# K turned by VectorE for other units, and q0 of four heads in two halves, in a sliding-window attention kernel

## The chip, the cores and the metric

The kernel runs on one core of a Trainium2 chip. A core has a matrix engine (TensorE, "PE" in the profile, its weight loads "PEld"), a vector engine (VectorE, "DVE"), a scalar engine (ScalarE, "ACT"), a general engine (GpSimd, "POOL") and a queue engine (SyncE, "SP") that issues nearly all transfers here. Transfers are carried by 16 DMA engines, which work beside the five. The engines run at the same time, each through its own instructions in order, and wait for each other by semaphores. SBUF is the memory on the core, PSUM the one that TensorE writes.

The metric is the time of one execution on the device, in microseconds (us). Eight executions of the kernel before lie between 185.21 and 186.71, with a median of 185.62.

## The reference

```python
B, Sq, D = 8, 32, 1024
Hq, Hkv, Sk, Dh = 32, 4, 8192, 128
W = 2048                                   # the last W positions of the cache
rep = Hq // Hkv                            # 8 query heads share one K and V
q = (x @ wq)  as [B, Hq, Sq, Dh]
k = k_cache[:, :, Sk - W:, :],  v = v_cache[:, :, Sk - W:, :]   each repeated rep times
p = softmax(q @ k^T * Dh**-0.5)
out = ((p @ v) as [B, Sq, Hq*Dh]) @ wo
```

All tensors are bf16. K and V of one batch entry and one KV head are 2048 x 128, 512 KB each.

## The kernel before

**Units and slots.** The work is cut into 32 units, one for each pair of KV head g and batch entry b: units 0 to 7 have g = 0, units 8 to 15 have g = 1, and so on. A unit has 256 queries (8 heads of 32) against 2048 keys. It is worked in four slots of 512 keys, so slot 4u is the first slot of unit u, and there are 128 slots. In a slot TensorE makes the scores (L467, four matmuls into s_ps), ScalarE takes their exponentials (L469, pT), and TensorE makes the product with V of a slot that lies two back (L478, eight matmuls into o_ps). V has a column of ones beside it in the tiles va, so that o_ps also holds the sum of the exponentials. At a unit's end VectorE takes the reciprocal of that sum (L415), scales o_ps (L420, two instructions of 128 columns) and transposes the result in blocks into OT (L422).

**Side work.** TensorE has other matmuls to do between these: q of the next KV head (q_pieces, L275, eight heads in 16 pieces), the output projection of a finished one (o_pieces, L295), and transposes of K. A dictionary, made by side_plan, says which piece is put behind which slot. Q_SLOTS and O_SLOTS give each group's first and last slot, and the function spread lays the pieces evenly over them. The order of every engine's instructions is the program's order.

**K comes turned in three ways.** The scores need K with its 128 columns on the partitions.

- Units in PE_T (0 to 4): K is loaded as it lies (L193) and turned by TensorE against an identity (L236, sixteen transposes in four pieces during the unit before, one piece behind each slot), then copied from PSUM by VectorE (L238). Unit 0's K is turned during the start (L368).
- Units in V_T (5, 8, 11, ... 29): K is loaded as it lies. VectorE transposes blocks of 32 x 32 (L251, four instructions), and sixteen moves of 32 partitions by 512 elements put the blocks in place. An entry holds the unit whose loading also loads this K, the slots of the four transposes, the first and last slot of the moves, and how many of the sixteen moves GpSimd makes (L261). VectorE makes the rest (L259). It is 12 for unit 5 and 16 for the others.
- All other units, 18 of them: a transposing DMA (L196), in two halves of 256 KB.

**Loads.** SP issues all of them in program order. load_unit loads a unit's K and V and then, where W_AT names this unit, pieces of wq or wo, in the order of the list self.weights. Loads are asked for about five units ahead; SP waits at an instruction until its target buffer is free. wq of one KV head comes in two tiles, each with half of the rows of the product's inner dimension and all eight heads; a DMA of 512 KB then has rows of 2 KB.

**The start.** x is loaded and transposed, q of KV head 0 (q0) is computed chunk by chunk as the chunks of wq land (L375): all 256 columns (8 batch entries of 32) for the first six chunks, and the first 128 columns for the last two. The 16 matmuls that are left are made behind slots 0 and 1 (q_rest). Four copies put the columns of batch entry 0 into QT (two by ScalarE, two by VectorE), four more by VectorE put the rest.

**V.** VectorE copies V of each unit from its landing tile into one of three tiles va (L409), at the unit's first slot.

Of the kernel before, what the change touches and what calls it, by code (L numbers as in the profile page):

```python
# [9 lines left out]
ALU = mybir.AluOpType  # L10
# [5 lines left out]

RL_LIMIT = 1.0e22
RL_MIN = 1.0e-10
Q_CUT = 6
N_WARM = (8, 0, 0)  # L20
VA_ROW = 160
V_HALVES = 30

PE_T = (0, 1, 2, 3, 4)

V_T = {5: (2, (5, 6, 8, 10), 10, 17, 12),
       **{u: (u - 4, range(4 * u - 16, 4 * u - 12), 4 * u - 13, 4 * u - 4, 16) for u in (8, 11, 14, 17, 20, 23, 26, 29)}}
W_AT = (3, 3, 4, 4, 8, 8, 9, 9, 11, 12, 13, 13, 14, 15, 16, 16, 18, 19, 19, 20, 22, 22, 23, 24, 25, 26, 28, 28)

Q_SLOTS = {1: (17, 31), 2: (38, 54), 3: (69, 83)}  # L30
O_SLOTS = {0: (54, 71), 1: (84, 101), 2: (99, 123), 3: (124, 143)}


# [71 lines left out]
class Fast:  # L105
# [50 lines left out]
    def load_wq(self, g, half, cuts=(2, 2)):  # L156
# [8 lines left out]
                                   in_=self.wq[:, g * GW:(g + 1) * GW].rearrange("(p c) n -> p c n", p=P)[:, c0:c0 + n, :])  # L165
        return [lambda i=sum(cuts[:k]), n=n: piece(i, n) for k, n in enumerate(cuts)]

    def load_wo(self, gq):

        def piece(i):  # L170
            if i == 0:
                self.wo_t[gq] = self.wp.tile([self.P, 4, self.D], BF16, name="wo_sb", tag="w")
            r0 = gq * 4 * self.Dh
            self.nc.sync.dma_start(out=self.wo_t[gq][:, 2 * i:2 * i + 2, :],
                                   in_=self.wo[r0:r0 + 4 * self.Dh, :].rearrange("(p c) n -> p c n", c=4)[:, 2 * i:2 * i + 2, :])
        return [lambda i=i: piece(i) for i in range(2)]
# [30 lines left out]
    def load_unit(self, ui):  # L207

        if ui < len(self.units):
            if ui not in V_T:  # L210
                self.load_k(ui, None if ui in PE_T else 0)
            self.load_v(ui, self.nc.sync)
            if ui not in V_T and ui not in PE_T:
                self.load_k(ui, 1)
        for u, at in V_T.items():
            if at[0] == ui:
                self.load_k(u)
        for p, at in zip(self.weights, W_AT):
            if at == ui:
                p()  # L220

# [17 lines left out]
    def kv_pieces(self, ui):  # L241


        nc, P, KT = self.nc, self.P, self.KT
        st = {}

        def blocks(i):
            if i == 0:
                st["kb"] = self.kbp.tile([P, KT, P], BF16, name="kb")
            sl = slice(i * KT // 4, (i + 1) * KT // 4)  # L250
            nc.vector.transpose(out=st["kb"][:, sl, :], in_=self.k_raw[ui][:, sl, :])  # L251

        def move(k, d):
            if k == d == 0:
                self.kT[ui] = self.kvt.tile([P, KT, P], BF16, name="kTv", tag="kv")
            out = self.kT[ui][d * 32:(d + 1) * 32, :, k * 32:(k + 1) * 32]
            in_ = st["kb"][k * 32:(k + 1) * 32, :, d * 32:(d + 1) * 32]
            if d >= V_T[ui][4] // 4:
                nc.vector.tensor_copy(out=out, in_=in_)  # L259
            else:  # L260
                nc.gpsimd.tensor_scalar(out=out, in0=in_, scalar1=1.0, scalar2=1.0, op0=ALU.mult, op1=ALU.mult)  # L261
        return [lambda i=i: blocks(i) for i in range(4)], [lambda k=k, d=d: move(k, d) for k in range(4) for d in range(4)]
# [4 lines left out]
    def q_pieces(self, g):  # L267
        nc, P, DC = self.nc, self.P, self.DC
        st = {}

        def piece(hl, i):
            if i == 0:
                st["ps"] = self.ps_m.tile([P, 512], FP32, name="q_ps", tag="m")
            for c in range(i * DC // 2, (i + 1) * DC // 2):
                nc.tensor.matmul(st["ps"][:, 0:self.NQ], lhsT=self.wq_t[g, i][:, c % (DC // 2), hl * P:(hl + 1) * P],  # L275
                                 rhs=self.xT[:, c, :], start=(c == 0), stop=(c == DC - 1))
            if i == 1:
                nc.vector.tensor_copy(out=self.q_view(g)[:, :, hl, :],  # L278
                                      in_=st["ps"][:, 0:self.NQ].rearrange("p (b s) -> p b s", b=self.B))
        return [lambda h=h, i=i: piece(h, i) for h in range(self.rep) for i in range(2)]  # L280

    def o_pieces(self, g, t, cuts=(512, 512), st=None):

# [28 lines left out]
    def start(self):  # L312
# [15 lines left out]
        self.load_k(0, 1)  # L328
        self.load_v(0, nc.sync)
        self.load_k(1)  # L330
        self.load_v(1, nc.sync)
        self.weights = []
        for g in range(self.Hkv):
            if g + 1 < self.Hkv:
                self.weights += self.load_wq(g + 1, 0) + self.load_wq(g + 1, 1)
            if g:
                self.weights += self.load_wo(2 * g - 2) + self.load_wo(2 * g - 1)
        self.weights += self.load_wo(2 * self.Hkv - 2) + self.load_wo(2 * self.Hkv - 1)
        for ui in range(2, 4):
            self.load_unit(ui)  # L340
        for v in self.va:
            nc.gpsimd.memset(v[:, :, self.Dh:self.VW], 1.0)
        nc.gpsimd.memset(self.ones_c[:, :], 1.0)
        def warm_up(n):
            for i in range(n):
                nc.tensor.matmul(warm[:, :], lhsT=one(1.0, [P, P], BF16), rhs=one(1.0, [P, 512], BF16), start=True, stop=True)
        warm_up(N_WARM[0])


        def x_turn(half, pl, tag):  # L350
# [4 lines left out]
            for i, copy in ((0, nc.vector.tensor_copy), (1, nc.scalar.copy)):  # L355
# [2 lines left out]

        x_turn(0, self.ps_m, "m")
        x_turn(1, self.ps_s, "s_ps")  # L360
        qs = [pl.tile([P, 2, self.NQ], FP32, name="q0_ps", tag=tag)
              for pl, tag in ((self.ps_o, "o_ps"), (self.ps_o, "o_ps"), (self.ps_m, "m"), (self.ps_m, "m"))]
        KT = self.KT
        tp = None

# [5 lines left out]
            sl = slice(half * KT // 2, (half + 1) * KT // 2)  # L371
            nc.vector.tensor_copy(out=self.kT[0][:, sl, :], in_=tp[:, sl, :])

        def q_mm(c, h, n0, n1):
            nc.tensor.matmul(qs[h // 2][:, h % 2, n0:n1], lhsT=self.wq_t[0, c // H][:, c % H, h * P:(h + 1) * P],  # L375
                             rhs=self.xT[:, c, n0:n1], start=(c == 0 and h % 2 == 0), stop=(c == self.DC - 1),
                             skip_group_check=True)

        for c in range(self.DC):
            for h in range(self.rep):  # L380
                q_mm(c, h, 0, P if c >= Q_CUT else self.NQ)
            if c == 0:
                warm_up(N_WARM[2])
                warm_sb = self.c1.tile([P, 8], BF16, name="warm_sb")
                nc.vector.tensor_copy(out=warm_sb[:, :], in_=warm[:, 0:8])
            if c == self.DC - 3:
                tp = self.ps_s.tile([P, KT, P], BF16, name="kf_ps", tag="s_ps")
                k_turn(0)
                k_copy(0)
        k_turn(1)  # L390

        def q_copy(eng, k, b0, b1):
            src = qs[k][:, :, :].rearrange("p h (b s) -> p b h s", b=self.B)[:, b0:b1, :, :]
            dst = self.q_view(0)[:, b0:b1, k * 2:(k + 1) * 2, :]
            (nc.vector.tensor_copy if eng == "v" else nc.scalar.copy)(out=dst, in_=src)
        for k, eng in ((0, "a"), (1, "v"), (2, "a"), (3, "v")):
            q_copy(eng, k, 0, 1)
        k_copy(1)
        self.va_copy(0)

        def q_rest(k):
            for h in (2 * k, 2 * k + 1):
                for c in range(Q_CUT, self.DC):
                    q_mm(c, h, P, self.NQ)
            q_copy("v", k, 1, self.B)
        self.q_rest = [lambda k=k: q_rest(k) for k in (0, 2, 3, 1)]

    def va_copy(self, ui):
        self.nc.vector.tensor_copy(out=self.va[ui % 3][:, :, 0:self.Dh], in_=self.v_sb[ui][:, :, :])  # L409

    def finish_unit(self, ui, o_ps):
        nc, P, Dh, QT_N = self.nc, self.P, self.Dh, self.QT_N
# [3 lines left out]
        if ui == len(self.units) - 1:  # L416
            self.check_units(ui, ui + 1)
        o_sb = self.ob.tile([P, QT_N, 4, 32], BF16, name="o_sb")
        for qt in range(QT_N):
            nc.vector.tensor_scalar(out=o_sb[:, qt, :, :], in0=o_ps[:, qt, 0:Dh].rearrange("p (i c) -> p c i", c=4),  # L420
                                    scalar1=rl[:, ui * QT_N + qt:ui * QT_N + qt + 1], scalar2=None, op0=ALU.mult)
        nc.vector.transpose(out=self.OT[:, g * QT_N:(g + 1) * QT_N, :, b * self.Sq:(b + 1) * self.Sq], in_=o_sb[:, :, :, :])  # L422
        if ui == len(self.units) - 2:
            self.check_units(0, ui + 1)
# [1 line left out]
    def side_plan(self):  # L426
# [4 lines left out]
        def spread(pieces, s0, s1):  # L431
            for k, p in enumerate(pieces):
                plan[s0 + (s1 - s0) * k // len(pieces)].append(p)
        for g, w in Q_SLOTS.items():
            spread(self.q_pieces(g), *w)
        for g, w in O_SLOTS.items():
# [8 lines left out]
    def run(self):  # L445
        nc, P, NCH, CJ, UQ, QT_N, KT = self.nc, self.P, self.NCH, self.CJ, self.UQ, self.QT_N, self.KT
        self.start()
        plan = self.side_plan()
        for i, p in enumerate(self.q_rest):
            plan[i // 2].append(p)  # L450
        pv_queue = []

        loads = {8: [4, 5, 6, 7], **{4 * (u - 5): [u] for u in range(8, len(self.units))}}
# [1 line left out]
        for ui, (b, g) in enumerate(self.units):  # L455
            nxt = self.k_pieces(ui + 1)
            va = self.va[ui % 3]
            if ui:
                self.va_copy(ui)
            q_u = self.QT[g][:, b * UQ:(b + 1) * UQ]  # L460
            acc = {}
            for c in range(NCH):
                for u in loads.get(ui * NCH + c, []):
                    self.load_unit(u)
                s_ps = self.ps_s.tile([P, CJ, UQ], FP32, name="s_ps")
                for jj in range(CJ):
                    nc.tensor.matmul(s_ps[:, jj, :], lhsT=self.kT[ui][:, c * CJ + jj, :], rhs=q_u, start=True, stop=True)  # L467
# [14 lines left out]
                pv_queue.append(pv)  # L482
                while len(pv_queue) > 2:
                    pv_queue.pop(0)()
                for k in ((c,) if ui else ((), (), (0, 1), (2, 3))[c]) if nxt else ():
                    nxt[k]()
                for p in plan[ui * NCH + c]:
                    p()
        after = [p for s in range(len(self.units) * NCH, len(plan)) for p in plan[s]]
# [166 lines left out]
```

## Time and profile before

| | |
|---|---|
| median of eight executions | 185.62 us |
| profiled execution | 185.24 us |
| its span, first to last instruction of the program | 183.5 us |
| granted TensorE clock | full, in all slices |
| start of slot 0's scores | 13.08 us |
| start of slot 127's scores | 172.46 us |
| DMA: moved in all | 51.72 MB |
| the last load lands | 167.27 us |

The span leaves out 1.74 us of the execution, which lie before its first and after its last instruction. The profile's page gives each engine's busy time, the same in 40 slices of the span, the costliest groups of instructions, and the transfers. A group's row gives its line, its engine and operation, the tile written and the tiles read, the shape, the count, and behind the bar the busy time and the mean duration of one instruction in ns; behind the second bar stands the idle time of the engine just before these instructions, and what ended it. The trace also has the start and landing of each transfer, and each DMA packet's size and time.

### The profile page before, as it was taken

Reading aid. Unit: us, or ns where it says so; the run is one execution under the profiler, and the core shown is the slowest. Engines: PE = TensorE matmul, PEld = TensorE weight load, DVE = VectorE, ACT = ScalarE, POOL = GpSimd, SP = SyncE. Lnnn points to the kernel's source line nnn. Section 1 sums busy time; section 2 is a strip of 40 time slices with the busy share of each in tenths; the row PEclk is TensorE's granted clock in tenths of the full one; section 3 lists DMA queues with packets and bytes.
Section 4 is the critical chain, followed back from the end, with each engine's and each line's share of the span. In section 5 each row is a group of like instructions: output and inputs, shape, how many; then the busy total and the mean of one; then the engine's idle time right before and its main releaser. Section 6 shows DMA issues by size and latency. Waiting matters only on the chain.

```text
span 183.5 us, 5041 instructions
## 1 busy us (share of the span) xinstructions
PE 178.6 (97%) x2041; PEld 153.5 (84%) x2057; DVE 115.0 (63%) x266; ACT 131.6 (72%) x133; POOL 94.9 (52%) x150
## 2 busy tenths in 40 slices
PE   8999999999999999999999999999999999999994
PEld 3789999999999999987878999988787888888843
DVE  0238899985585784685567558647755865365363
ACT  2218999777789777878787677787877888888800
POOL 2000009759939959929945980796299279600000
PEclk9999999999999999999999999999999999999999
DMA  5999999999999999999999999999999989990003
GB/s 191 328 411 404 401 403 384 203 222 375 268 342 278 317 309 322 400 252 256 364 380 239 346 397 238 221 329 386 262 364 337 237 244 308 217 220 1 0 31 91
DMA packets 52953, 51.72 MB, mean 282 GB/s; under 512 B 39744, under 2 KB 40256, under 8 KB 52928
## 3 DMA queue, kind: packets, MB, share of 16 engines
q1 hardware_dynamic: 52352, 50.90, 98.2%
q10 hardware_dynamic: 576, 0.49, 0.8%
q8 instruction: 15, 0.25, 0.5%
q14 instruction: 10, 0.08, 0.1%
HBM read 41.42 MB, written 0.52 MB: 229 GB/s over the span
## 4 chain that ended last, share of the span: by engine, by line
PE 93%; DMA 3%; SPq 1%; issue 1%; DVE 0%
PE o_ps L478 32%; PE s_ps L467 31%; PE op_ps L295 14%; PE q_ps L275 11%; DMA wq_sb<-in_wq_dram 3%; PE q_ps L375 2%; PE tp L236 2%; SPq L164 1%; PE kf_ps L368 1%; SPq L320 0%; DVE o_t L305 0%; PE cnt_ps L532 0%
## 5 line engine op out<-in xcount | busy, mean ns | idle before, releaser
L469 ACT ACTIVATE pT<-s_ps 128x1024 bf16<-128x1024 f32 x128 | 128.8, 1025 | 32.5 <-PE s_ps L467 31.6
L261 POOL TENSOR_SCALAR kTv<-kb 32x512 bf16<-32x512 bf16 x140 | 94.0, 671 | 63.8 <-PE s_ps L467 37.4
L478 PE MATMUL o_ps<-va,pT 128*128 128x129 bf16 x1024 | 78.8, 220 | 0.1
L478 PEld LDWEIGHTS <-pT 128*128 128x128 bf16 x1024 | 68.5, 98 | 3.1
L467 PE MATMUL s_ps<-QT,kT 128*128 128x256 bf16 x368 | 55.2, 272 | 0.2
L467 PEld LDWEIGHTS <-kT 128*128 128x128 bf16 x368 | 34.8, 98 | 10.3
L295 PE MATMUL op_ps<-wo_sb,OT 128*128 128x512 bf16 (+2 forms) x128 | 32.7, 352 | 0.6
L275 PE MATMUL q_ps<-xT,wq_sb 128*128 128x256 bf16 x192 | 28.1, 273 | 0.0
L409 DVE COPY va<-v_sb 128x2048 bf16<-128x2048 bf16 x32 | 25.5, 795 | 0.1
L251 DVE STREAM_TRANSPOSE kb<-k_raw 128x512 bf16<-128x512 bf16 x36 | 23.8, 684 | 0.0
L415 DVE RECIPROCAL RL_all<-o_ps 128x2 f32<-128x2 f32 x32 | 5.2, 164 | 27.4 <-PE o_ps L478 27.3
L467 PE MATMUL s_ps<-QT,kTv 128*128 128x256 bf16 x144 | 21.6, 272 | 0.0
L420 DVE TENSOR_SCALAR o_sb<-o_ps,RL_all 128x128 bf16<-128x128 f32 x64 | 19.5, 347 | 1.1
L278 DVE CAST QT<-q_ps 128x256 bf16<-128x256 f32 x24 | 9.8, 406 | 13.4 <-PE q_ps L275 13.4
L467 PEld LDWEIGHTS <-kTv 128*128 128x128 bf16 x144 | 13.9, 98 | 5.1
L275 PEld LDWEIGHTS <-wq_sb 128*128 128x128 bf16 x192 | 17.0, 98 | 1.2
L422 DVE STREAM_TRANSPOSE OT<-o_sb 128x256 bf16<-128x256 bf16 x32 | 14.3, 446 | 1.1
L295 PEld LDWEIGHTS <-OT 128*128 128x128 bf16 x144 | 11.4, 98 | 2.3 <-DVE OT L422 0.2
L302 DVE TENSOR_TENSOR oacc<-op_ps,oacc 128x512 f32<-128x512 f32 x8 | 5.5, 682 | 7.4 <-PE op_ps L295 7.4
L375 PE MATMUL q_ps<-xT,wq_sb 128*128 128x256 bf16 (+1 forms) x80 | 7.9, 251 | 0.5 <-DMA wq_sb<-in_wq_dram 0.5
L375 PEld LDWEIGHTS <-wq_sb 128*128 128x128 bf16 x80 | 6.5, 98 | 1.5 <-DMA wq_sb<-in_wq_dram 0.9
L236 PE MATMUL tp<-ident,k_raw 128*128 128x128 bf16 x64 | 5.9, 219 | 0.0
(30 smaller groups left out, 36.4 us busy)
## 6 DMA issues: line engine op xcount, KB each, us to landing
v_sb<-in_v_cache_dram SPq DMA_DIRECT2D x30, 512.0 KB, 7.1
wo_sb<-in_wo_dram SPq DMA_DIRECT2D x16, 512.0 KB, 7.0
wq_sb<-in_wq_dram SPq DMA_DIRECT2D x13, 512.0 KB, 7.3
k_raw<-in_k_cache_dram SPq DMA_DIRECT2D x13, 512.0 KB, 6.3
wq_sb<-in_wq_dram SPq DMA_DIRECT2D x6, 256.0 KB, 4.8
v_sb<-in_v_cache_dram SPq DMA_DIRECT2D x4, 256.0 KB, 5.5
kT<-in_k_cache_dram SPq DMA_TRANSPOSE x36, 6.8
k_raw<-in_k_cache_dram SPq DMA_DIRECT2D x2, 256.0 KB, 6.6
```

What stands on the lines that cost most here:

```text
L251: nc.vector.transpose(out=st["kb"][:, sl, :], in_=self.k_raw[ui][:, sl, :])
L261: nc.gpsimd.tensor_scalar(out=out, in0=in_, scalar1=1.0, scalar2=1.0, op0=ALU.mult, op1=ALU.mult)
L275: nc.tensor.matmul(st["ps"][:, 0:self.NQ], lhsT=self.wq_t[g, i][:, c % (DC // 2), hl * P:(hl + 1) * P], rhs=self.xT[:, c, :], start=(c == ...
L278: nc.vector.tensor_copy(out=self.q_view(g)[:, :, hl, :], in_=st["ps"][:, 0:self.NQ].rearrange("p (b s) -> p b s", b=self.B))
L295: nc.tensor.matmul(ps[:, 0:w], lhsT=self.OT[:, gq, c, t * P:(t + 1) * P], rhs=self.wo_t[gq][:, c, n0:n0 + w], start=(k == 0), stop=(k == 7))
L375: nc.tensor.matmul(qs[h // 2][:, h % 2, n0:n1], lhsT=self.wq_t[0, c // H][:, c % H, h * P:(h + 1) * P], rhs=self.xT[:, c, n0:n1], start=(c ...
L409: self.nc.vector.tensor_copy(out=self.va[ui % 3][:, :, 0:self.Dh], in_=self.v_sb[ui][:, :, :])
L420: nc.vector.tensor_scalar(out=o_sb[:, qt, :, :], in0=o_ps[:, qt, 0:Dh].rearrange("p (i c) -> p c i", c=4), scalar1=rl[:, ui * QT_N + qt:ui ...
L422: nc.vector.transpose(out=self.OT[:, g * QT_N:(g + 1) * QT_N, :, b * self.Sq:(b + 1) * self.Sq], in_=o_sb[:, :, :, :])
L467: nc.tensor.matmul(s_ps[:, jj, :], lhsT=self.kT[ui][:, c * CJ + jj, :], rhs=q_u, start=True, stop=True)
L469: nc.scalar.activation(out=pT[:, :, :], in_=s_ps[:, :, :], func=ACT.Exp, bias=0.0, scale=self.scale)
L478: nc.tensor.matmul(o_ps[:, qt, 0:self.VW], lhsT=pT[:, jj, qt * P:(qt + 1) * P], rhs=va[:, j, 0:self.VW], start=(j == 0 and qt == 0), stop= ...
```

## The change

- PE_T becomes units 0 to 2. V_T becomes 4, 7, 10, 12, 15, 17, 20, 22, 25, 27 and 29, eleven units for nine. Unit 3 now comes by transposing DMA, and so do 5, 8, 11, 14, 23 and 26; units 7, 10, 12, 15, 22, 25 and 27 no longer do. Transposing DMA has 18 units as before.
- GpSimd makes 9 of the 16 moves for unit 4, and 12 for the other units; VectorE's share is spread evenly among the sixteen.
- V of units 1 and 2 is copied by GpSimd. V of unit 3 is copied in slot 9, not at its own first slot; from unit 12 on, V is copied in the last slot of the unit before.
- q0: heads 0 to 3 are computed for all 256 columns during the start, heads 4 to 7 for the first 128 columns. Their other 128 columns come from q_late, 32 matmuls in four pieces behind slots 0, 1, 8 and 10. The copies into QT become three for batch entry 0, three for the rest of these columns, and two for q_late.
- wq of KV heads 1 to 3 comes in two tiles of four heads each; a DMA of 512 KB then has rows of 1 KB. q_pieces puts two heads in one PSUM tile, and ScalarE copies both at once (four copies of 512 elements for each g) where VectorE made eight. Q_SLOTS of KV head 1 begins at slot 14, not 17.
- The scaling at a unit's end is one tensor_tensor with the reciprocals broadcast, not two instructions.
- The K pieces of TensorE stand behind slots 1, 2 and 3 of the unit before (one, one and two), not one behind each of the four.
- load_unit issues the weights ahead of the K of later units; the first loads are reordered to V1, K2, K4, V2, and then unit 3.

```diff
-PE_T = (0, 1, 2, 3, 4)
-V_T = {5: (2, (5, 6, 8, 10), 10, 17, 12),
-       **{u: (u - 4, range(4 * u - 16, 4 * u - 12), 4 * u - 13, 4 * u - 4, 16) for u in (8, 11, 14, 17, 20, 23, 26, 29)}}
-W_AT = (3, 3, 4, 4, 8, 8, 9, 9, 11, 12, 13, 13, 14, 15, 16, 16, 18, 19, 19, 20, 22, 22, 23, 24, 25, 26, 28, 28)
-Q_SLOTS = {1: (17, 31), 2: (38, 54), 3: (69, 83)}
+PE_T = (0, 1, 2)
+V_T = {4: (None, (4, 6, 6, 7), 8, 15, 9),
+       7: (4, (15, 16, 17, 18), 18, 26, 12),
+       10: (6, (25, 26, 27, 28), 28, 37, 12),
+       **{u: (u - 4, range(4 * u - 14, 4 * u - 10), 4 * u - 11, 4 * u - 2, 12) for u in (12, 15, 17, 20, 22, 25, 27, 29)}}
+W_AT = (3, 3, 5, 5, 8, 8, 10, 10, 11, 12, 13, 13, 14, 15, 17, 17, 18, 19, 19, 20, 22, 22, 23, 24, 25, 26, 28, 28)
+Q_LATE = {0: (0, 2), 1: (8, 12)}
+V_EARLY = 12
+V_AT = {3: 9}
+Q_SLOTS = {1: (14, 31), 2: (38, 54), 3: (69, 83)}
...
+    def load_wq_heads(self, g, half):
+        P, DC, GW = self.P, self.DC, self.rep * self.Dh
+        n0 = g * GW + half * GW // 2
+        def piece(i):
+            if i == 0:
+                self.wq_t[g, half] = self.wp.tile([P, DC, GW // 2], BF16, name="wq_sb", tag="w")
+            cs = slice(i * DC // 2, (i + 1) * DC // 2)
+            self.nc.sync.dma_start(out=self.wq_t[g, half][:, cs, :],
+                                   in_=self.wq[:, n0:n0 + GW // 2].rearrange("(p c) n -> p c n", p=P)[:, cs, :])
+        return [lambda i=i: piece(i) for i in range(2)]
...
-            if d >= V_T[ui][4] // 4:
+            i, n = 4 * k + d, 16 - V_T[ui][4]
+            if i * n // 16 != (i + 1) * n // 16:
                 nc.vector.tensor_copy(out=out, in_=in_)
...
+            if i == 1 and hl % 2 == 1:
+                nc.scalar.copy(out=self.q_view(g)[:, :, 2 * k:2 * k + 2, :].rearrange("p b h s -> p h b s"),
+                               in_=st["ps"][:, :, :].rearrange("p h (b s) -> p h b s", b=self.B))
...
+    def q_late(self, h0):
...
+            for c in range(DC):
+                nc.tensor.matmul(st["ps"][:, i, :], lhsT=self.wq_t[0, c // (DC // 2)][:, c % (DC // 2), (h0 + i) * P:(h0 + i + 1) * P],
+                                 rhs=self.xT[:, c, P:self.NQ], start=(c == 0 and i == 0), stop=(c == DC - 1), skip_group_check=True)
...
         for c in range(self.DC):
-            for h in range(self.rep):
-                q_mm(c, h, 0, P if c >= Q_CUT else self.NQ)
...
+            for h in range(self.rep):
+                q_mm(c, h)
...
     def va_copy(self, ui):
-        self.nc.vector.tensor_copy(out=self.va[ui % 3][:, :, 0:self.Dh], in_=self.v_sb[ui][:, :, :])
+        out, in_ = self.va[ui % 3][:, :, 0:self.Dh], self.v_sb[ui][:, :, :]
+        if ui in (1, 2):
+            self.nc.gpsimd.tensor_scalar(out=out, in0=in_, scalar1=1.0, scalar2=1.0, op0=ALU.mult, op1=ALU.mult)
+        else:
+            self.nc.vector.tensor_copy(out=out, in_=in_)
...
-        for qt in range(QT_N):
-            nc.vector.tensor_scalar(out=o_sb[:, qt, :, :], in0=o_ps[:, qt, 0:Dh].rearrange("p (i c) -> p c i", c=4),
-                                    scalar1=rl[:, ui * QT_N + qt:ui * QT_N + qt + 1], scalar2=None, op0=ALU.mult)
+        nc.vector.tensor_tensor(out=o_sb[:, :, :, :], in0=o_ps[:, :, 0:Dh].rearrange("p q (i c) -> p q c i", c=4),
+                                in1=rl[:, ui * QT_N:(ui + 1) * QT_N].unsqueeze(2).unsqueeze(3).to_broadcast([P, QT_N, 4, 32]), op=ALU.mult)
...
-            if ui:
+            if 0 < ui < V_EARLY and ui not in V_AT:
                 self.va_copy(ui)
...
-                for k in ((c,) if ui else ((), (), (0, 1), (2, 3))[c]) if nxt else ():
-                    nxt[k]()
+                for k in ((), (0,), (1,), (2, 3))[c] if ui else ((), (), (0, 1), (2, 3))[c]:
+                    if nxt:
+                        nxt[k]()
```

## The prediction

> **What bounds the kernel now.** I read the page first: busy shares, the 40 slices, the groups of instructions.
>
> ```profile
> span 183.5 us, 5041 instructions
> ...
> PE 178.6 (97%) x2041; PEld 153.5 (84%) x2057; DVE 115.0 (63%) x266; ACT 131.6 (72%) x133; POOL 94.9 (52%) x150
> ...
> DMA  5999999999999999999999999999999989990003
> ...
> L469 ACT ACTIVATE pT<-s_ps 128x1024 bf16<-128x1024 f32 x128 | 128.8, 1025 | 32.5 <-PE s_ps L467 31.6
> L261 POOL TENSOR_SCALAR kTv<-kb 32x512 bf16<-32x512 bf16 x140 | 94.0, 671 | 63.8 <-PE s_ps L467 37.4
> ...
> L420 DVE TENSOR_SCALAR o_sb<-o_ps,RL_all 128x128 bf16<-128x128 f32 x64 | 19.5, 347 | 1.1
> ...
> L236 PE MATMUL tp<-ident,k_raw 128*128 128x128 bf16 x64 | 5.9, 219 | 0.0
> ```
>
> TensorE is busy throughout, the other engines wait for it, and no group of matmuls waits as much as 1 us. But a second row is full too: the DMA engines stand at 9 until shortly before the end. So I asked for stages of the trace (columns: engine busy us with counts, granted clock, DMA share, GB/s) and for the DMA of one stage.
>
> ```profile
> 18.00:32.00 14.00, 14.00 (x203) 13.37 (x202) 12.94 (x29) 12.59 (x13) 4.44 (x7) 1.00 1.07 397
> 32.00:60.00 28.00, 28.00 (x347) 26.18 (x344) 19.96 (x48) 22.68 (x24) 20.66 (x31) 1.00 1.16 282
> 60.00:90.00 30.00, 29.89 (x346) 26.39 (x346) 19.54 (x46) 23.27 (x23) 22.49 (x35) 1.00 1.13 312
> 90.00:130.00 40.00, 39.74 (x448) 34.27 (x452) 26.86 (x60) 30.13 (x30) 24.84 (x38) 1.00 1.12 321
> ```
>
> ```profile
> DMA packets 10347, 7.90 MB, mean 282 GB/s; under 512 B 8415, under 2 KB 8415, under 8 KB 10342
> ```
>
> From 18 to 32 us plain loads alone run, at 397 GB/s: a 512 KB tile takes 1.32 us. From 32 to 60 us transposing loads are mixed in (their packets are the 8415 of 256 B) and the rate falls to 282. Those packets are 2.15 MB; the other 5.75 MB take 14.5 us at 397 GB/s, which leaves 13.5 us for 8.2 halves: 1.65 us a half, **3.3 us for a unit's K by transposing DMA against 1.32 plain**. The same sum gives 2.8 us in each of the next two stages. DMA is a second bound, just ahead of TensorE.
>
> How far ahead? In the trace's DMA records unit 9's K landed at 50.2 and 52.4 us; the timeline of TensorE shows its use (the first row is slot 36, the unit's first; the third slot 38, which takes the second half):
>
> ```profile
> 55.86 0.60 PE L467 MATMUL s_ps<-QT,kT 128*128 128x256 bf16 x4
> 56.29 0.62 PE L478 MATMUL o_ps<-va,pT 128*128 128x129 bf16 x8
> ...
> 57.69 0.60 PE L467 MATMUL s_ps<-QT,kT 128*128 128x256 bf16 x4
> ```
>
> So it has 5.3 us in hand. Other units have 4 to 8.
>
> **The change, part by part.** Slots are read off the starts of s_ps: a bare slot lasts 0.89 us, one with four K transposes 1.11, one with a q piece 1.33.
>
> *TensorE.* Units 3 and 4 lose their 32 transposes: 8 pieces of 1.11-0.89 = 0.22, -1.76 us. Of q0, 16 half-width matmuls ran in slots 0 and 1; now 32 run, in slots 0, 1, 8 and 10. Eight took 0.44 us, so +0.88 there. The start runs fewer columns, but waits for wq: the fifth chunk landed at 9.44 and slot 0 began at 13.08. Between lay 16 wide matmuls (1.9), 8 transposes (0.44), 16 narrow (0.88), 8 transposes. Now it is 8 wide and 8 narrow (1.35), 8 transposes, 8 wide and 8 narrow (1.35), 8 transposes: some 0.1 shorter. The copies behind it are three instead of four, the last one wider; from the 213 ns of the 64-element ACT copy I bound this end by 0.2 either way. Sum -0.98. Spreading g1's q pieces from slot 14 moves work and adds none.
>
> *Unit's end.* Two L420 (0.61 us together) become one tensor_tensor. The trace lacks it; the nearest row, L305 128x256 from PSUM, took 426 ns. Only the last unit's lies on the path, where L295 waited 0.2 us for OT: -0.2 (0 to -0.2).
>
> *q copies to ScalarE.* Twelve copies of 128x512; half of L469's 1025 ns, 0.5 us, is the nearest. An exp ended 1.72 us after its slot's s_ps began, and the slot that needs its PSUM begins at 2.66: 0.94 of cover, so 0. Without cover each would cost some 0.5, 6 in all. DVE sheds their 9.8 us, and takes 47 moves instead of 4 (0.45 each, +19) and 8 more block transposes (0.68, +5.5): still under 75% busy.
>
> *V1, V2 on GpSimd.* Not in the trace; L261 moves 512 elements a partition in 671 ns, so 2048 take 2.7 us (2.0 if part of it is fixed). V1 landed at 15.97: ready 18.7, used in slot 6 at 19.9. V2, one place later at 20.8: ready 23.5, used in slot 10 at 24.6. Hidden, by 1.1 us each.
>
> *Unit 4 by VectorE.* K4 lands near 19.5. Its four blocks (0.68 each) stand between unit 2's PSUM copies and unit 0's end and finish near 24.2. Then 9 GpSimd moves; unit 5's twelve took 27.19 to 35.98, 0.73 each with the V copies beside them: 6.6, ready at 30.8. Slot 16 begins at 30.9. Cost 0, with no cover to speak of; up to +1. Later units have 12 moves (8.8 us) for at least 10.6 us between units: hidden.
>
> *V copies one slot early, from unit 12.* 0: pv uses V two slots on. A late V now blocks DVE; behind it are moves and a reciprocal that have two slots or more.
>
> *DMA.* As many units as before, 18, come transposed, but of units 0 to 9 it was 6, 7 and 9, and now it is 3, 5, 6, 8 and 9. SP's queue goes in order: the issue of a transposed half held it for 1.2 to 5.4 us in the trace, and V3 and wq of g1 are now queued behind unit 3's. The DMA engines had work all that while, so I count this inside the 3.3. And twelve wq tiles now have rows of 1 KB instead of 2 KB: the trace's packets took 48 and 84 ns (medians), so 32x48 against 16x84 per engine, 1.54 against 1.34: +0.19 each.
>
> Now unit 9's second half. Before, K of 11 units came first or with it, three of them transposed; after, 12, five transposed. One more tile +1.3, two more transposed +4.0, six wq tiles +1.1: it lands at 52.4+6.4 = **58.8**. TensorE wants it at 57.69-0.98 = 56.7. It waits 2.1, and is 1.1 later than before. At unit 14 I compare with unit 15's first half (landed 81.82): a V and a wq less (-2.6), one more transposed (+2.0), eight wq (+1.5): 82.7, where slot 56 began at 81.56: also 1.15 later than before. From there to unit 31 counts even out (the last K: +2.3 for wq, against 3.9 in hand). What follows slot 56 on TensorE is unchanged.
>
> **A rule against a row.** The Trainium skill, "DMA: Bandwidth & Descriptors", section "Latency and other measured facts", gives DMA transposes an effective 261 GB/s in the non-contiguous case. That makes 2.0 us a unit, +0.7 over plain: unit 9 would land at 52.4+1.3+1.4+1.1 = 56.2, before it is wanted, and nothing would wait. This trace's 3.3 (2.8 at the least) is the price here, stalls between plain and transposing loads included; I take the row. With 2.8 unit 9 still lands at 57.8, 0.1 later than before, and unit 14 at 82.2, 0.65 later.
>
> **Sum.** The profiled execution took 185.24 us, 1.74 outside its span. +1.15 at unit 14, -0.2 at the end: 186.2. The median of the eight runs is 0.38 above that execution, so **186.6**.
>
> **Rivals.**
> *DMA keeps up (rule's price).* For it: 4 to 8 us in hand, and the transposes are as many in all. Against: the stages above. Then TensorE's sum stands: 185.24-0.98-0.2 = 184.1, as a median 184.4 (faster). It decides from where unit 9's K lands before 56.7, a unit at 2.25 us.
> *DMA falls further behind.* Before, some transposed units followed each other and shared a stall (6 and 7, 12 and 13); now nearly each stands alone after plain loads, with more packets queued. At 3.8 us a unit, unit 9 lands at 59.8 and, with eight transposed units (against six, at 3.3) in front, unit 14 some 3 later than before: 185.24+3-0.2 = 188.0, median 188.4.
> *Unit 4 sets the pace.* DMA keeps up but GpSimd's moves end 0.9 late at slot 16: 184.1+0.9 = 185.0, median 185.4. For it: no cover. Against: 0.73 a move already holds the V copies.
>
> **How the numbers follow.** Forecast 0.46 (185.9 to 187.6), DMA keeps up 0.26 (184.1 to 185.2), further behind 0.20 (187.6 to 190), unit 4 0.08. A measurement can tell 0.5% from nothing: under 184.7 is faster, over 186.55 slower. Faster: four fifths of the second case, 0.20. Same: the rest of it, unit 4, and a third of the forecast, 0.29. Slower 0.51. The range, 184.2 to 188.8, leaves out a few hundredths below and a tenth above.
>
> **What would show it.** Right: tp falls to 32 matmuls; s_ps or o_ps of units 9 and 14 wait on DMA kT for about 2 us in sum; GB/s between 18 and 60 us falls, with 256 B packets from 20 us on; slots of units 2 and 3 last near 0.9. Wrong: no wait of TensorE on kT (the rule's price), a wait at slot 16 on POOL kTv, or exps that start late behind the q copies.

## The result and the profile after

| | before | after |
|---|---|---|
| median of all executions | 185.69 us (58) | 186.92 us (21) |
| ratio after to before | | 1.0065, 95% interval 1.0043 to 1.0086 |
| profiled execution, its span | 185.24, 183.5 us | 187.15, 185.4 us |
| start of slot 0, slot 127 | 13.08, 172.46 us | 13.00, 174.21 us |

The kernel is slower by 0.4 to 0.9%: 1.2 us by the ratio. The two profiled executions lie 1.9 apart, because that of before is 0.45 below its median and that of after 0.2 above; the points below are read from this pair.

The page of the kernel after: busy shares, the DMA row of the 40 slices, and groups of instructions.

```profile
PE 178.3 (96%) x2025; PEld 152.7 (82%) x2041; DVE 123.8 (67%) x255; ACT 135.9 (73%) x145; POOL 90.9 (49%) x141
...
DMA  5999999999999999999999999999999999970013
...
L508 PE MATMUL s_ps<-QT,kT 128*128 128x256 bf16 x336 | 50.4, 272 | 2.0 <-DMA kT<-in_k_cache_dram 1.7
...
L508 PE MATMUL s_ps<-QT,kTv 128*128 128x256 bf16 x176 | 26.4, 272 | 0.4 <-DVE kTv L277 0.4
...
L456 DVE TENSOR_TENSOR o_sb<-o_ps,RL_all 128x256 bf16<-128x256 f32 x32 | 13.6, 424 | 1.1
...
L444 POOL TENSOR_SCALAR va<-v_sb 128x2048 bf16<-128x2048 bf16 x2 | 3.8, 1897 | 17.3 <-DMA v_sb<-in_v_cache_dram 17.3
L297 ACT CAST QT<-q_ps 128x512 bf16<-128x512 f32 x12 | 7.0, 581 | 0.0
```

No compute engine has become the bound, and the DMA row is as full as before. New is that matmuls of scores wait: 1.7 us on DMA, 0.4 us on VectorE. The stages again (columns as before: stretch; busy us of PE, PEld, DVE, ACT, POOL; granted clock, DMA share, GB/s):

```profile
18.00:32.00 14.00, 14.00 (x195) 13.12 (x193) 12.50 (x27) 12.13 (x13) 8.64 (x11) 1.00 1.14 285
32.00:60.00 28.00, 26.28 (x324) 24.25 (x322) 20.08 (x41) 23.48 (x27) 15.70 (x24) 1.00 1.17 285
60.00:90.00 30.00, 29.47 (x341) 25.98 (x341) 20.40 (x42) 24.29 (x27) 16.71 (x25) 1.00 1.13 315
90.00:130.00 40.00, 39.74 (x449) 34.38 (x453) 28.54 (x59) 31.52 (x35) 23.54 (x35) 1.00 1.11 329
```

From 18 to 32 us the rate has fallen from 397 to 285 GB/s; later stages stand as before. TensorE pays for it one stage later: its 28.00 us between 32 and 60 are now 26.28. Its timeline around slots 36 to 38:

```profile
55.35 0.61 PE L508 MATMUL s_ps<-QT,kT 128*128 128x256 bf16 x4 [0.18 <-DMA kT<-in_k_cache_dram]
...
56.25 0.60 PE L508 MATMUL s_ps<-QT,kT 128*128 128x256 bf16 x4
56.69 0.62 PE L519 MATMUL o_ps<-va,pT 128*128 128x129 bf16 x8
58.84 0.61 PE L508 MATMUL s_ps<-QT,kT 128*128 128x256 bf16 x4 [1.54 <-DMA kT<-in_k_cache_dram]
```

Slot 36 waits for the first half of unit 9's K and slot 38 for the second, which lands at 58.80. Slot 38 starts 1.15 later than before. Slot 56, unit 14's first, does too (82.72 against 81.56). Then comes a wait that the forecast did not have. Slots 59 and 60 in TensorE's timeline:

```profile
86.69 0.60 PE L508 MATMUL s_ps<-QT,kT 128*128 128x256 bf16 x4
...
88.60 0.60 PE L508 MATMUL s_ps<-QT,kTv 128*128 128x256 bf16 x4 [0.43 <-DVE kTv L277]
```

And the chain of waits from 76 to 89 us (start, duration, what):

```profile
76.00 7.91 DMA v_sb<-in_v_cache_dram
...
83.93 0.72 DVE va L446
...
84.67 0.59 DVE kTv L277
...
85.28 1.30 DVE kb L268 x2
...
86.67 0.44 DVE o_sb L456
...
87.13 0.45 DVE OT L458
87.58 0.57 DVE oacc L334
...
88.16 0.30 DVE kTv L277
...
88.60 0.60 PE s_ps L508 x4
```

V of unit 14 lands at 83.90. Its copy, which the change puts one slot earlier, stood at the head of VectorE's queue for 2.2 us. Everything behind it was late, down to the last move of unit 15's K, and slot 60 needs that move: the step from slot 59 to 60 is 1.91 us where it was 1.32 before (85.53 to 86.85). That is +0.59, and from slot 60 to slot 127 the delay stays at 1.75.

Where the rate fell is seen in the DMA rows of the stretch from 18 to 32 us, in 40 slices of 0.35 us. Before:

```profile
GB/s 386 445 398 410 410 398 421 398 421 380 375 386 392 392 380 415 392 375 410 386 392 416 410 433 398 421 380 398 416 369 392 386 380 386 404 404 404 415 368 319
```

After:

```profile
GB/s 339 245 132 64 50 23 12 207 396 328 374 410 303 290 290 413 354 351 345 345 339 351 351 483 374 372 374 375 374 492 303 294 89 23 23 17 274 452 374 386
```

Two holes, at about 18.7 to 20.4 and 29.2 to 30.6 us, with the rate down to 12 and 17 GB/s. Each ends about 1.1 us before the first half of a transposed unit lands (unit 3 at 21.61, unit 5 at 31.69). Between the holes most slices stand between 290 and 410 GB/s.

### The profile page after: what moved, and what is told of

Read it like the earlier page. It is cut to its first block, busy times and chain, and to the rows that moved or that the text cites. A ratio compares the mean times of both kernels' runs of the same rounds, so it can differ in the third digit from the quotient of the medians.

```text
span 185.4 us, 5017 instructions
## 1 busy us (share of the span) xinstructions
PE 178.3 (96%) x2025; PEld 152.7 (82%) x2041; DVE 123.8 (67%) x255; ACT 135.9 (73%) x145; POOL 90.9 (49%) x141
## 4 chain that ended last, share of the span: by engine, by line
PE 80%; DMA 12%; DVE 4%; SPq 1%; issue 1%
PE o_ps L519 27%; PE s_ps L508 27%; PE op_ps L329 13%; PE q_ps L294 10%; DMA kT<-in_k_cache_dram 4%; DMA v_sb<-in_v_cache_dram 4%; DMA wq_sb<-in_wq_dram 3%; PE q_ps L412 2%; PE tp L253 1%; PE ql_ps L309 1%; SPq L168 1%; DVE kb L268 1%; DVE o_sb L456 1%; PE kf_ps L404 0%; DVE OT L458 0%
## 5 line engine op out<-in xcount | busy, mean ns | idle before, releaser
L279 POOL TENSOR_SCALAR kTv<-kb 32x512 bf16<-32x512 bf16 x129 | 86.2, 668 | 52.4 <-DVE kb L268 33.0
L508 PE MATMUL s_ps<-QT,kT 128*128 128x256 bf16 x336 | 50.4, 272 | 2.0 <-DMA kT<-in_k_cache_dram 1.7
L508 PEld LDWEIGHTS <-kT 128*128 128x128 bf16 x336 | 31.7, 98 | 11.7 <-DMA kT<-in_k_cache_dram 2.3
L268 DVE STREAM_TRANSPOSE kb<-k_raw 128x512 bf16<-128x512 bf16 x44 | 29.5, 691 | 1.5 <-DMA k_raw<-in_k_cache_dram 1.1
L508 PE MATMUL s_ps<-QT,kTv 128*128 128x256 bf16 x176 | 26.4, 272 | 0.4 <-DVE kTv L277 0.4
L508 PEld LDWEIGHTS <-kTv 128*128 128x128 bf16 x176 | 16.9, 98 | 6.8 <-issue 0.9
L277 DVE COPY kTv<-kb 32x512 bf16<-32x512 bf16 x47 | 20.4, 434 | 1.1
L456 DVE TENSOR_TENSOR o_sb<-o_ps,RL_all 128x256 bf16<-128x256 f32 x32 | 13.6, 424 | 1.1
L444 POOL TENSOR_SCALAR va<-v_sb 128x2048 bf16<-128x2048 bf16 x2 | 3.8, 1897 | 17.3 <-DMA v_sb<-in_v_cache_dram 17.3
L297 ACT CAST QT<-q_ps 128x512 bf16<-128x512 f32 x12 | 7.0, 581 | 0.0
```

What stands on the lines that cost most here:

```text
L456: nc.vector.tensor_tensor(out=o_sb[:, :, :, :], in0=o_ps[:, :, 0:Dh].rearrange("p q (i c) -> p q c i", c=4), in1=rl[:, ui * QT_N:(ui + 1) ...
```

## The experiments

Edits are against the kernel after, except in the third and fourth, which are against the kernel before. Ratios are to the kernel before, with 95% intervals.

**V at its own slot again.**

```diff
-V_EARLY = 12
+V_EARLY = 99
```

> The changed kernel with V of every unit from 4 on copied at the unit's own first slot again (V_EARLY = 99). Theory A (the second loss, 0.59 us before slot 60, comes from VectorE standing at V of unit 14 with the last K move of unit 15 queued behind): slot 60 starts within 0.1 us of its bare time after slot 59, the wait of unit 9 stays (slot 38 at 58.8 us), span 184.8 to 185.0. Rival B (unit 15's K itself was late, or GpSimd's moves): the gap before slot 60 stays at about 0.6 us and the span at 185.4.

Measured: 1.0074 [1.0046, 1.0103], span 185.6. Slot 60's wait is gone (86.64 to 87.96, step 1.32), and unit 9's is not: slot 38 begins at 58.79, and most of the 2.2 us of waiting now falls on slot 36. So the early copies cause the one and not the other. But the expected span was missed: the gain is given back at slots 107 and 108, which take 1.01 more than in the kernel after. The chain there:

```profile
147.26 0.69 DVE oacc L336
...
147.96 0.72 DVE kTv L277
...
148.69 0.71 DVE kb L268
149.41 1.03 DVE va L446
...
150.48 0.61 PE o_ps L519 x8
```

Now V's copy stands behind other work of VectorE and the product with V waits 0.6 us for it. The early copy moves a wait, from V itself to what stands behind V.

**Unit 3 turned by TensorE again**: one transposing load becomes a plain one.

```diff
-PE_T = (0, 1, 2)
+PE_T = (0, 1, 2, 3)
```

> The changed kernel with unit 3's K turned by TensorE again, all else kept. Theory A (the transposing load of unit 3 takes about 2 us more of the DMA engines than a plain one, and this is what makes unit 9 late): unit 9's second half lands near 56.8 us instead of 58.8, TensorE does not wait for it, V of unit 14 lands before 82 us and slot 60 does not wait either; TensorE has 0.88 us more work; span 183.7 to 184.0. Rival B (a transposing load costs 0.7 us more than a plain one, the page's rate): unit 9's second half lands at 58.1, a wait of 0.3 us or less is left because TensorE comes later, and V of unit 14 lands at 83.2. Rival C (DMA is late for the 1 KB rows or the order of loads): the landing stays within 0.5 us of 58.8.

Measured: 1.0016 [0.9999, 1.0033], span 184.6. Unit 9's second half landed at 57.34, 1.46 earlier, and slots 36 and 38 wait for no load. So the price of one transposing load over a plain one, by this landing, lies between the row's 2.0 and the rule's 0.7. The load explains about three quarters of the 2 us of waiting; the rest went because TensorE itself came to slot 35 later, at 55.38 instead of 54.12. Of this 0.88 was expected. The step from slot 11 to 12, with two pieces of transposes, took 1.93 instead of 1.33, and 0.4 of the difference is recorded as K's transposes waiting for VectorE's copy of the piece before. V of unit 14 landed at 82.99, not before 82, and slot 60 waited 0.60 as in the kernel after. These two put the span above the expected 183.7 to 184.0.

**wq in rows of 1 KB, alone**, in the kernel before.

```diff
+            if g:
+                n0, h0 = i * GW // 4, half * self.DC // 2
+                self.nc.sync.dma_start(out=self.wq_t[g, half][:, :, n0:n0 + GW // 2],
+                                       in_=self.wq[:, g * GW + n0:g * GW + n0 + GW // 2].rearrange("(p c) n -> p c n", p=P)[:, h0:h0 + self.DC // 2, :])
+                return
```

> The kernel before with the twelve later wq tiles loaded in rows of 1 KB (column halves) instead of 2 KB, same tiles, same count and size of transfers. Theory A (0.19 us more for each tile): unit 9's second K half, behind six such tiles, lands 1.1 us later than in the kernel before, near 53.5; it has 5 us in hand, so the time is the same within 0.3%. Rival B (row length costs nothing, other traffic hides it): it lands within 0.4 us of 52.4.

Measured: 1.0011 [0.9991, 1.0031]. Counted from V2's landing, unit 9's K is 0.78 later after six such tiles, 0.13 each, where 0.19 was predicted. The mechanism holds at two thirds of its size, and alone it costs no time: before, that K had 5 us in hand.

**Unit 3 by transposing DMA, alone**, in the kernel before.

```diff
-PE_T = (0, 1, 2, 3, 4)
+PE_T = (0, 1, 2, 4)
```

> The kernel before with unit 3's K by transposing DMA instead of TensorE, all else kept. Theory A: TensorE loses 16 transposes, 0.88 us, from slots 8 to 11, and unit 9's second K half lands about 2 us later, near 54.4, still 2.4 us ahead of its use: span 182.6 to 182.8, ratio 0.995 to 0.996. Rival B (ScalarE or another engine takes over in the bare slots, so that nothing is gained): span 183.3 or more. Rival C (the page's rate): the landing moves by 0.7 us, to 53.1.

Measured: 1.0162 [1.0122, 1.0203], span 187.8. TensorE's saving came, 0.85 of the expected 0.88: slots 8 to 11 took 3.60 instead of 4.45. But the gain in time did not. TensorE's timeline, with the scores of slots 12 and 13 in the first and last row:

```profile
25.84 0.60 PE L467 MATMUL s_ps<-QT,kT 128*128 128x256 bf16 x4
...
29.71 0.47 PE L236 MATMUL tp<-ident,k_raw 128*128 128x128 bf16 x4 [2.82 <-DMA k_raw<-in_k_cache_dram]
29.97 1.06 PE L467 MATMUL s_ps<-QT,kT 128*128 128x256 bf16 x4
```

Raw K of unit 4, three places behind in SP's queue, landed at 29.66 instead of 27.39, and TensorE begins to turn it at 27.4 in the kernel before: a load with no cover, which the expectation did not count. The wait then cost more than its 2.8 us. From 30 to 33 us the granted clock was 0.50, and four matmuls of scores took 1.06 us instead of 0.60; slots 12 to 15 lost 4.57 in all, so 1.8 beside the wait. Another execution of this kernel kept the mean clock at 1.000 and had a span of 185.4, which is what the wait alone would give (183.5 - 0.9 + 2.8).

Unit 9's K landed 1.27 later. V of unit 2, which lands ahead of the changed load, was itself 0.36 late in this execution; counted from there, unit 4's K is 1.9 late and unit 9's 0.9. So one more transposing load shifts the loads behind it by 0.9 to 1.9. In the changed kernel unit 4's K is loaded ahead of unit 3's and lands at 19.39, so the wait of this run does not arise there.

**q copies on VectorE again.**

```diff
-                nc.scalar.copy(out=self.q_view(g)[:, :, 2 * k:2 * k + 2, :].rearrange("p b h s -> p h b s"),
+                nc.vector.tensor_copy(out=self.q_view(g)[:, :, 2 * k:2 * k + 2, :].rearrange("p b h s -> p h b s"),
```

> The changed kernel with the twelve q copies of KV heads 1 to 3 on VectorE again. If they cost nothing on ScalarE, as the prediction has it, the span stays at 185.4 within 0.3 us, unless VectorE's queue delays unit 15's K further: it makes two such copies there no more (q of head 2 ends at slot 54), so not. If ScalarE's copies delayed exps that TensorE waits for, the span falls by up to 1 us.

Measured: 1.0083 [1.005, 1.0116], span 185.4, as after. Which engine copies q decides nothing for the time. The waits lie differently, though: the waits for unit 9's K are 0.7 shorter in sum than in the kernel after, and slot 56 waits 0.60 for the first half of unit 14's K, which landed at 82.84. Unit 14 has no cover either.

**V of units 1 and 2 on VectorE again.**

```diff
-        if ui in (1, 2):
+        if ui in ():
```

> The changed kernel with V of units 1 and 2 copied by VectorE again. VectorE gets two copies of 0.7 us between slots 4 and 9, where its blocks of unit 4 and PSUM copies of unit 2 stand: unit 2's or unit 4's K comes up to 1.5 us later and TensorE waits there. Unit 9's second half still lands at 58.8 us, so this wait is made up by a shorter one at slot 38, and the span stays within 0.4 us of 185.4. Rival (delays add): span 186.2 or more.

Measured: 1.014 [1.0112, 1.0168], span 186.3: worse than I expected, and what the rival said. Slot 16 waits 0.60 instead of 0.16, unit 9's K lands at 59.48, V of unit 14 at 85.04, and slot 60 waits 1.03 in the same chain as above. A part that was counted at nothing is worth about 1 us (186.3 less 185.4). Why the loads land 0.7 and 1.1 later was not separated; V of unit 2 already landed 0.38 later in that execution.

**Other units for VectorE.** If unit 9's late K is the cause, the remedy is to let VectorE turn units 9 and 14 instead of 10 and 15, with as many units on each way as before.

```diff
-       10: (6, (25, 26, 27, 28), 28, 37, 12),
-       **{u: (u - 4, range(4 * u - 14, 4 * u - 10), 4 * u - 11, 4 * u - 2, 12) for u in (12, 15, 17, 20, 22, 25, 27, 29)}}
+       **{u: (u - 4, range(4 * u - 14, 4 * u - 10), 4 * u - 11, 4 * u - 2, 12) for u in (9, 12, 14, 17, 20, 22, 25, 27, 29)}}
```

> The changed kernel with units 9 and 14 turned by VectorE instead of 10 and 15 (V_T of 4, 7, 9, 12, 14, 17, 20, 22, 25, 27, 29); still 18 transposed units. Theory A (TensorE's own sum is 0.98 us shorter, and the loss is unit 9's and unit 14's loads coming too late): neither slot 36 nor 38 nor 60 waits; unit 6's halves land 1.3 us later but still in time, unit 11's within 0.5 us of their use; span 182.8 to 183.4, ratio to the kernel before 0.995 to 0.998. Rival B (DMA as a whole is what bounds, so a wait only moves): the wait comes back at unit 10 or 11 with more than 1 us, span 184.5 or more.

Measured: 0.9978 [0.9958, 0.9999], span 183.8. No load is waited for at slots 36 and 38, and slot 60 does not wait. Slot 36 still begins 0.27 late, now for GpSimd's last move of unit 9's K. New is a wait of 0.61 us at slot 46: the second half of unit 11's K lands at 68.62, behind the wq pieces of unit 10.

```profile
68.67 0.61 PE L507 MATMUL s_ps<-QT,kT 128*128 128x256 bf16 x4 [0.44 <-DMA kT<-in_k_cache_dram]
```

**A denser choice** of units.

```diff
-       10: (6, (25, 26, 27, 28), 28, 37, 12),
-       **{u: (u - 4, range(4 * u - 14, 4 * u - 10), 4 * u - 11, 4 * u - 2, 12) for u in (12, 15, 17, 20, 22, 25, 27, 29)}}
+       **{u: (u - 4, range(4 * u - 14, 4 * u - 10), 4 * u - 11, 4 * u - 2, 12) for u in (9, 11, 14, 17, 19, 22, 24, 27, 29)}}
```

> As the run with 9 and 14 by VectorE, and also 11, 19 and 24 instead of 12, 20 and 25 (4, 7, 9, 11, 14, 17, 19, 22, 24, 27, 29). Theory A: unit 11's transposing load is gone from the tight stretch; no wait on loads over 0.3 us, span 182.8 to 183.2. Rival (GpSimd's and VectorE's work for three units two apart, 8 us of moves in 10.6 us each, is too dense): s_ps waits on kTv at slot 36 or 44.

Measured: 1.0054 [1.0033, 1.0074], span 184.9. In time up to slot 60, then the steps to slots 64 and 68 take 2.1 us each instead of 1.32. Slot 64 waits for the first half of unit 16's K. The wait at slot 68 has the chain of slot 60 of the kernel after, with a later V at its head. The wait of slot 64, then the chain of slot 68:

```profile
PE s_ps L507 <- DMA kT<-in_k_cache_dram: 0.6, 1, 0.6
...
88.62 5.61 DMA v_sb<-in_v_cache_dram
...
94.25 0.69 DVE va L445
...
98.90 0.60 PE s_ps L507 x4
```

The expected 182.8 to 183.2 was missed, and the rival's sign, s_ps waiting for kTv, came at slot 68 instead of 36 or 44. But both waits begin with a late load, so its reason, moves that are too dense, is not shown.

**The wait of slot 46.** As with units 9 and 14, and the wq pieces of unit 10 issued with unit 11.

```diff
-W_AT = (3, 3, 5, 5, 8, 8, 10, 10, 11, 12, 13, 13, 14, 15, 17, 17, 18, 19, 19, 20, 22, 22, 23, 24, 25, 26, 28, 28)
+W_AT = (3, 3, 5, 5, 8, 8, 11, 11, 11, 12, 13, 13, 14, 15, 17, 17, 18, 19, 19, 20, 22, 22, 23, 24, 25, 26, 28, 28)
```

> As f1_shift, with the second half of the third head's W_q loaded after unit 11's K instead of before it. Theory A (TensorE waits only for the load that comes last): unit 11's second K half lands about 1.5 us earlier, the 0.61 us of waiting at slot 46 goes, and the rest of the timetable stays: span about 183.2, ratio to the kernel before 0.994 to 0.997. Rival (the wait changes hands): the first q of the third head, due at slots 46 and 47, now waits for the W_q half that lands after the K, TensorE waits about as long as before: span 183.8, ratio 0.998.

Measured: 0.9977 [0.9954, 1.0], median 185.15 us against 185.84, span 183.0. TensorE waits for no load after the start (the 0.27 at slot 36 is GpSimd's move, as in the run with units 9 and 14), and slot 127 begins at 172.04, 0.42 before the kernel before although slot 0 begins 0.27 after it. The median is 0.5 below that of the version that waits at slot 46, but the two ratios, taken on two chips, can't be told apart; against the kernel before it is 0.2% faster at an interval that just reaches 1.

**One move less for GpSimd at unit 4**, on top of that.

```diff
-V_T = {4: (None, (4, 6, 6, 7), 8, 15, 9),
+V_T = {4: (None, (4, 6, 6, 7), 8, 15, 8),
```

> As g1_wq_later, with GpSimd taking 8 instead of 9 of the block moves of unit 4. Theory A (at slot 16 TensorE waits for GpSimd's last move): the wait of 0.27 us at slot 16 falls to about 0, span 0.2 to 0.3 us below g1_wq_later's, ratio 0.993 to 0.996. Rival (VectorE's last move of that unit ends at about the same time, and now gets one more of 0.3 us): the wait stays or grows to 0.4, span equal to g1_wq_later's or 0.2 above.

Measured: 0.9987 [0.9964, 1.0009], span 183.9. The rival was right that the wait grows:

```profile
PE s_ps L507 <- DVE kTv L276: 0.5, 1, 0.5
```

VectorE's last move of unit 4 now begins at 31.5 instead of 30.3 and slot 16 waits for that; another 0.4 us went at slot 8, where the scores waited for an exp. The two ratios, with 8 moves and with 9, can't be told apart. With 9 moves the same slot waited 0.16, 0.27 and 0 in three runs: it has no cover, as the forecast said, and a few tenths between executions decide.

## Why the prediction was right, and where not

The median was forecast at 186.6 and is 186.9; the mechanism, unit 9's K landing late after DMA lost its lead, is the one forecast. That the number came so close is in part luck. The sum missed 0.59 at slot 60 and took off 0.2 at the end that does not exist, 0.8 in all; the median is only 0.3 above the forecast because the medians lie 1.2 apart and the two profiled executions 1.9.

- **TensorE's sum, -0.98: right.** Slot 35 begins at 54.12 instead of 54.94. That is -0.82 after a wait of 0.16 at slot 16, so -0.98 without it.
- **Unit 9, right in its time, not in its terms.** Predicted 58.8, landed at 58.80; waits of 2.1 predicted, 0.31 + 1.67 measured by the steps between slots; slot 38 later by 1.1 predicted, 1.15 measured. But of the +6.4 the wq term was 0.8 rather than 1.1, and the term of 2.0 for a transposed unit is not one number: it was 1.5 where one was taken away, 0.9 to 1.9 where one was added, and the change itself leaves 4.3 for two (6.4 less 1.3 for the tile and 0.8 for wq). The exact hit owes something to luck.
- **Rule or row.** The Trainium skill ("DMA: Bandwidth & Descriptors", "Latency and other measured facts") gives DMA transposes 261 GB/s in its non-contiguous case; the estimate from this figure put unit 9 at 56.2, and it landed 2.6 later. The runs put a transposing load at 0.9 to 2.2 us over a plain one: always above the rule's 0.7, mostly below the row's 2.0. The holes show what a mean rate leaves out: for about 1.5 us, ending 1.1 before the first half of such a load lands, hardly anything moves.
- **Unit 14, right.** 82.7 predicted, 82.59 landed; slot 56 is 1.16 later, as unit 9 had left it.
- **"A late V now blocks DVE; behind it are moves and a reciprocal that have two slots or more": wrong.** I priced this at 0, and it cost 0.59. Behind V's copy stood 4.5 us of VectorE's work, from 83.9 to 88.5, and its last piece was a move that slot 60 needed. The chain above shows it, and the run with V at its own slot takes it away there.
- **The end, -0.2: wrong, it is 0.** The 0.2 of waiting for OT was that of a weight load, which runs ahead; the matmuls behind it were back to back before as well. The tensor_tensor itself took 424 ns for the 426 taken from the nearest row.
- **Copies.** q on ScalarE: 581 ns for the estimated 500, no exp of TensorE's path late, and no change when undone: right. V on GpSimd: 1.90 us for 2.7 (with the fixed part it was 2.0), hidden: right. That taking them back costs 1 us was not seen.
- **Two readings of the profile before.** "Other units have 4 to 8" us in hand: unit 10 had 3.0 and 3.4. And from 18 to 32 us it was not plain loads alone: 203 of the 2221 packets there were of 256 B, the start of unit 6's first half. Neither changes the sum.
- **The rivals.** "DMA keeps up" did not come. Where loads are made to keep up, with the wq pieces issued later, a third of its gain is reached: a ratio of 0.9977, where 184.4 would be 0.993. Of the 1.18 us that it counted, 0.2 at the end does not exist, 0.27 goes at slot 36, and slot 0 began 0.27 late in that execution. "Further behind" did not come. "Unit 4 sets the pace" came at 0.16 of its 0.9.

Left open: why the two more transposed units moved unit 9 by 4.3 us together where taking one away gave 1.5, and how the first V copies bear on the landing times. A V copy on an engine with nothing due behind it was not tried.

## What to carry to other kernels

When work is moved off an engine onto loads, count the landing time of the load that is needed first, not the busy share: 0.98 us saved by TensorE were lost to one K half that came 2 us late, and exchanging units between the ways of turning K won that back. Before an instruction that waits for DMA is put earlier in an engine's queue, add up what stands behind it until the first thing that another engine needs. Here it was 4.5 us; the early place of the copy cost 0.59 us and the late one 1.01. And price a wait by what follows it too: a gap of 2.8 us in TensorE's work cost 1.8 more at half the clock.

## What was not expected of the hardware

- In the stretch shown, the DMA rate fell below 100 GB/s for some 1.4 us (four slices of 0.35), down to 12 GB/s, ahead of the first half of both transposed units. The second half of unit 3, which also followed a plain load, had no such hole. In each hole 19 packets of 256 B lasted 0.9 to 2.1 us, where the median is 18 ns, and ended within 0.05 us of each other.
- After a wait of 2.8 us TensorE's granted clock was 0.50 for about 3 us (unit 3 alone by transposing DMA). After the wait of 1.54 us in the kernel after it stayed at 1.00.
- Moves of one size differ in time while GpSimd and VectorE work side by side: 32 x 512 took GpSimd 0.61 to 0.95 us and VectorE 0.28 to 0.66, among unit 4's moves in the run with units 9 and 14 on VectorE. VectorE's two longest, 0.66, began 0.1 us after a move of GpSimd's had begun; a move that began 0.1 before one ended took 0.28.
- A 512 KB tile in 1 KB rows took 0.13 us more than in 2 KB rows, in the mean of six.
